# A Fourier mixing layer with one routed token, on one core: an eighth raw tile, gathered last rows, odd folds on ScalarE, one-element writes between comparisons, and a table of priorities

## The chip, the cores and the metric

The kernel runs on one core of one Trainium2 chip. The core has five engines that run their own instruction queues beside each other: TensorE (PE, matrix products; PEld is its weight load), VectorE (DVE), ScalarE (ACT), GpSimd (POOL) and SyncE (SP, which only issues transfers here). Transfers are moved by 16 DMA engines that all queues share. The metric is the device time of one launch in microseconds (us), lower is better; the figure to beat is the median of three runs.

## The reference

Everything is float32. `x` is 2048 x 576, the two sequence matrices are 2048 x 2048 (cosine and sine), the two hidden ones 576 x 576, and the three weights of the feed-forward part are 576 x 4608.

```python
def _A_ref(x, seq_re, seq_im, hid_re, hid_im):          # Fourier mixing
    a = einsum("bsd,ed->bse", x, hid_re)
    b = einsum("bsd,ed->bse", x, hid_im)
    return einsum("ts,bse->bte", seq_re, a) - einsum("ts,bse->bte", seq_im, b)

def _B_ref(x, w_r, w_gate, w_up, w_down):               # one routed token
    r = x @ w_r
    idx = argsort(-r)[:, :1]                             # the token with the highest score
    x_sel = take(x, idx)
    y = (silu(x_sel @ w_gate) * (x_sel @ w_up)) @ w_down
    y = y * sigmoid(r[idx])
    return x + scatter(zero, idx, y)

h = x + _A_ref(layernorm(x), ...)
out = h + _B_ref(layernorm(h), ...)
```

The matrices are inputs, and the kernel may not assume that they are cosines and sines. It computes the product by their symmetries (a mirrored half), and checks on the chip that the symmetries hold for the matrices it was given; if they don't, a general path at the end runs (it does not run here).

## The kernel before

**Stages.** Sixteen slots of 128 tokens lie in `X`. Stage one folds each pair of slots k and 16-k into sums and differences along the hidden axis (`fold_d`, DVE), takes the layer norm's statistics (`measure` on ACT, `ends`, `totals`, `biases` on POOL, `scales` on DVE), and brings the pair together and normalizes it by two matmuls with diagonal matrices (`diag` on DVE, `fold` on PE). `folded` writes the result from PSUM to `XF`: the even half on ACT, the odd half on DVE (L548). Stage two (`seq`, PE) multiplies `XF` by the sequence matrices, in two groups of row blocks, five products for each group; `keep` turns the sums into `Z`. Stage three (`hid`, PE) multiplies `Z` by the hidden matrices. `residual` (DVE) adds x, `spread_of` (ACT) and `dot_h` (DVE) take the second norm and the router's score, `scores` finishes a batch of blocks, `result` writes the rows that are not routed, and `store` sends them out. Then comes the token: the highest score is found over all rows (`argmax`), its row is spread to all partitions (`to_all`, `normalized`), and the weights of the feed-forward part are streamed past it. `products` on DVE, `products_on_pool` on POOL with `sums` on ACT, and `products_only` share the gate and up weights, `down` (PE) takes the down weights. The down weights of the last three blocks are the last three loads.

**The checks.** Beside this every tile of the sequence matrices is compared with its mirror image. Direct tiles come by SP (`load_c`, L357, 576 KB each), mirrored ones by an indirect DMA of POOL (L301, 448 KB). A check (`c_check`) takes up to three comparisons on DVE: `off_s` (L375, 128x896, twice) and `off_t` (L380, 128x1152); `off_h` (L387) compares halves within the resident tiles `D0`, `D1`, `D2`. Each writes differences to one of two buffers `Q`, and ACT squares and sums a buffer (L368). The hidden matrix is checked in the same way: `W` holds three tiles (rows 0 to 127, 128 to 255, and in tile C 33 last rows and 32 more), loaded by SP at L403 and L405, mirrored by POOL, compared by `off_w` (L422 to L427).

**Buffers.** Tiles that only a check needs go to `RAW`, seven buffers of 4.5 KB per partition, and to those units of `D0`, `D1`, `D2` that are free at the time. The diagonal matrices have a tile of their own, `DGT` (L196). A buffer is loaded again once DVE has compared what it holds. In the last stage the same memory makes 16 spots of 1152 KB for weights.

**What sets the order.** The program is recorded into a `Plan`: each step has an engine, a length in us, and the steps it depends on. `order` runs a list schedule over the lengths: an engine takes, of the steps that are ready, the one with the longest way to the end (`way`) plus a bonus (`push`). The instructions are then issued in that order, and each engine's queue keeps it on the chip whatever really comes first. Loads are issued in a fixed order on SP and on POOL, each behind the load before it.

Of the kernel before, what the change touches and what calls it, by code (L numbers as in the profile page):

```python
# [1 line left out]

# [53 lines left out]
N_RAW = 7  # L56
# [3 lines left out]
N_PLAN = 6  # L60

# [9 lines left out]
class Plan:  # L71
# [14 lines left out]

    def order(self):
        HOP = 0.15
        succ = [[] for _ in self.ops]
        for n in self.ops:  # L90
            for d in n["deps"]:
                succ[d["i"]].append(n)
        for n in reversed(self.ops):
            n["way"] = n["dur"] + n["tail"] + max((m["way"] for m in succ[n["i"]]), default=0.0)
        left = [len(n["deps"]) for n in self.ops]
        open_ = {}
        for n in self.ops:
            n["at"] = 0.0
            if not n["deps"]:
                open_.setdefault(n["eng"], []).append(n)  # L100
        free = {}
        done = []
        while any(open_.values()):
            best = None
            for eng, ns in open_.items():
                if not ns:
                    continue
                t = max(free.get(eng, 0.0), min(n["at"] for n in ns))
                n = min(
                    (n for n in ns if n["at"] <= t + 1e-9),  # L110
                    key=lambda n: (n["at"] if eng == "DMA" else -n["way"] - n["push"], n["i"]),
                )
                if best is None or t < best[0]:
                    best = (t, n)
            t, n = best
            open_[n["eng"]].remove(n)
            n["start"], n["end"] = t, t + n["dur"]
            free[n["eng"]] = n["end"]
            done.append(n)
            for m in succ[n["i"]]:  # L120
                hop = 0.0 if m["eng"] == n["eng"] else HOP
                m["at"] = max(m["at"], n["end"] + n["tail"] + hop)
                left[m["i"]] -= 1
                if not left[m["i"]]:
                    open_.setdefault(m["eng"], []).append(m)
        assert len(done) == len(self.ops)
        return sorted(done, key=lambda n: (n["start"], n["i"]))
# [15 lines left out]
def kernel(  # L143
# [37 lines left out]
    mp = main.enter_context(tc.tile_pool(name="main", bufs=1))  # L181


    ident = consts.tile([P, P], F32, name="ident")
    ones = consts.tile([P, P], F32, name="ones")
# [10 lines left out]
    DGT = mp.tile([P, N_DG * P], F32, name="diag")  # L196
# [6 lines left out]
    iw = consts.tile([P, 3], I32, name="iw")  # L203
# [4 lines left out]
    dve.memset(ones, 1.0)  # L208
# [5 lines left out]
    def index_tables():  # L214
        pool.iota(ji, pattern=[[1, P]], base=0, channel_multiplier=-1)
        pool.iota(ic, pattern=[[2 * P, NK], [1, 2]], base=2 * (P - 1), channel_multiplier=-2)
        pool.iota(iw, pattern=[[-P, 3]], base=D, channel_multiplier=-1)
# [11 lines left out]
    def unit_matrix():  # L229
# [67 lines left out]
    ctv = ct.rearrange("j p i k m -> (j p i) (k m)")  # L297

    def gather(tile, view, rows, at=0):

        pool.indirect_dma_start(  # L301
            tile, None, view, bass.IndirectOffsetOnAxis(ap=rows, axis=0), element_offset=at
        )
# [3 lines left out]
    bufp = main.enter_context(tc.tile_pool(name="bufs", bufs=1))  # L307

    def buf(b, shape, dtype, name):
        return bufp.tile(shape, dtype, tag=f"b{b}", name=name, bufs=1)  # L310

# [7 lines left out]
    RAW = buf("R", [P, N_RAW, 9, P], F32, "R")  # L319
# [51 lines left out]

    def off_s(j, i, u, n):

        o = Q[:, u % 2, n * 7 * P : (n + 1) * 7 * P].rearrange("p (k m) -> p k m", m=P)
        dve.tensor_tensor(o, C[j, i, True][:, 0:7, :], C[j, i, False][:, 7:0:-1, :], op=SIGN[i])  # L375

    def off_t(j, i, u):

        o = Q[:, u % 2, 14 * P : QW].rearrange("p (k m) -> p k m", m=P)
        dve.tensor_tensor(o, C[NK - j, i, False], C[j, i, False][:, :, ::-1], op=SIGN[i])  # L380

    def off_h(g, c, n, i, u):
# [3 lines left out]
        for k, op in enumerate((OP.subtract, OP.add)):  # L386
            dve.tensor_tensor(o[:, :, k::2, :], t[:, :, k::2, 0:HM], t[:, :, k::2, HM:P], op=op)  # L387

    def square(u, w, ps=P):
        add_square(Q[0:ps, u % 2, 0:w])  # L390
# [26 lines left out]
    def off_w(n, u):  # L417

        ps = W_ROWS[n]
        t, o = WM["ABC"[n]][0:ps], Q[0:ps, u % 2]  # L420
        re, im = W["ABC"[n]][0:ps, 0, :], W["ABC"[n]][0:ps, 1, :]
        dve.tensor_tensor(o[:, 0:D], t[:, 0:D], re[:, 0:D], op=OP.subtract)  # L422
        dve.tensor_tensor(o[:, D : 2 * D], t[:, D : 2 * D], im[:, 0:D], op=OP.add)
        o = o[:, 2 * D : 3 * D]
        dve.tensor_tensor(o[:, 0:287], re[:, 1:HD], re[:, D - 1 : HD : -1], op=OP.subtract)
        dve.tensor_tensor(o[:, 287:575], im[:, 1 : HD + 1], im[:, D - 1 : HD - 1 : -1], op=OP.add)
        dve.tensor_copy(o[:, 575:576], im[:, 0:1])  # L427

    W_ROWS = (P, P, 33)
# [109 lines left out]
    def folded(k, part):  # L539
# [7 lines left out]
        else:  # L547
            dve.tensor_scalar(XF[:, q, O0 + 1 : O0 + 288], o[:, :287], sc, None, op0=OP.mult)  # L548
# [955 lines left out]
```

## Time and profile before

| | before |
|---|---|
| three runs | 200.21, 201.22 and 205.07 us |
| median | 201.22 us |
| the profiled execution | 201.27 us |
| its span, first to last instruction | 199.2 us |
| bytes moved | 77.81 MB |
| granted TensorE clock, mean | 0.858 |

The profiled execution is 0.05 us above the median, and 2.07 us longer than its span. In the profile the line of an instruction names the helper that recorded it, so L301 is every gather and L368 every square. "SPq" and "POOLq" are the queues that issue transfers. The tenths of the page's second part are shares of 40 equal slices of 5 us.

### The profile page before, as it was taken

To read this page: it belongs to the slowest core of one execution; us is meant where nothing else is said; L and a number is where in the kernel's file an instruction comes from. 1 tells how busy PE (TensorE), PEld (TensorE's weight loads), DVE (VectorE), ACT (ScalarE), POOL (GpSimd) and SP (SyncE) were. 2 spreads that over 40 slices of the span, in tenths; PEclk is the share of its full clock that TensorE was granted. 3 is DMA by queue.
4 is the path that set the end of the run, shared out by engine and by line. 5 is a ranking of instruction groups with operands and counts; after the bars stand their busy time and mean duration, and the time that the engine had idled before them with its cause. 6 is when DMAs were issued, how large, how long until landed. Compare 5 with 4: busy or idle time off the path is not lost. (4 is left out here: it accounts for less than half of the span.)

```text
span 199.2 us, 2787 instructions
## 1 busy us (share of the span) xinstructions
PE 130.4 (65%) x758; PEld 89.9 (45%) x758; DVE 166.1 (83%) x419; ACT 140.5 (71%) x259; POOL 122.8 (62%) x134
## 2 busy tenths in 40 slices
PE   0007989999999989899999996600241444085840
PEld 0005667764767778677877774400121111043220
DVE  4389997989999859997999999999839997899410
ACT  2298863783987794799587599997629999786400
POOL 6578888495528878998870000006439999998500
PEclk9999999999999999999999999985555555555798
DMA  5999999999979999999999999999999999999991
GB/s 190 361 418 415 411 411 409 409 372 346 402 275 366 415 398 391 404 407 412 407 401 418 420 420 422 427 414 423 422 428 425 428 422 420 431 420 412 422 387 42
DMA packets 14491, 77.81 MB, mean 391 GB/s; under 512 B 1855, under 2 KB 1859, under 8 KB 11143
## 3 DMA queue, kind: packets, MB, share of 16 engines
q1 hardware_dynamic: 10463, 56.56, 70.8%
q0 software_dynamic: 4000, 21.03, 26.3%
q8 instruction: 7, 0.11, 0.2%
q14 instruction: 13, 0.11, 0.1%
q10 hardware_dynamic: 8, 0.00, 0.0%
HBM read 72.86 MB, written 6.49 MB: 398 GB/s over the span
## 5 line engine op out<-in xcount | busy, mean ns | idle before, releaser
L368 ACT ACTIVATE Q<-Q 128x2944 bf16<-128x2944 bf16 (+5 forms) x26 | 55.4, 2133 | 19.9 <-DVE Q L375 7.0
L610 PE MATMUL py<-W,Z 128*128 128x289 f32 x180 | 45.3, 408 | 2.3 <-DVE X L619 2.3
L565 PE MATMUL ps<-D,XF 128*128 128x320 f32 (+3 forms) x216 | 45.0, 408 | 1.2 <-DMA D<-in_ct_dram 0.8
L301 POOL DMA_INDIRECT R<-in_ct_dram,ic x21 | 34.1, 1625 | 14.5 <-DVE Q L375 10.5
L610 PEld LDWEIGHTS py<-W,Z 128*128 128x128 f32 x180 | 33.7, 189 | 13.6 <-issue 2.9
L565 PEld LDWEIGHTS ps<-D,XF 128*128 128x128 f32 (+1 forms) x216 | 32.1, 172 | 13.8 <-issue 2.5
L1201 POOL TENSOR_TENSOR D<-D,Z 128x1152 f32<-128x1152 f32 x8 | 20.8, 2618 | 1.2 <-SPq L1331 1.2
L667 POOL DMA_DIRECT2D out_dram<-X x1 | 0.6, 606 | 30.0 <-ACT X L661 30.0
L301 POOL DMA_INDIRECT D<-in_ct_dram,ic x11 | 16.1, 1468 | 3.4 <-issue 2.4
L498 ACT ACTIVATE junk<-X,XT 128x576 bf16<-128x576 f32 x16 | 12.4, 772 | 8.0 <-DVE W L459 6.5
L1206 ACT ACTIVATE junk<-D 128x576 bf16<-128x576 f32 x20 | 13.7, 683 | 4.0 <-POOLq L1331 2.3
L1228 PE MATMUL pd<-XF,H 128*1 128x144 f32 x80 | 5.3, 440 | 16.1 <-DVE H L1220 13.3
L537 PE MATMUL fo<-W,diag 128*128 128x288 f32 (+1 forms) x8 | 3.9, 665 | 16.4 <-DVE diag L528 16.4
L387 DVE TENSOR_TENSOR Q<-D 128x640 bf16<-128x640 f32 (+3 forms) x20 | 12.7, 691 | 1.4 <-DMA D<-in_ct_dram 1.4
L380 DVE TENSOR_TENSOR Q<-R,D 128x1152 bf16<-128x1152 f32 x10 | 13.4, 1349 | 0.0
L630 ACT ACTIVATE junk<-X,TD 128x576 bf16<-128x576 f32 x16 | 12.3, 768 | 1.5 <-DVE X L619 1.3
L375 DVE TENSOR_TENSOR Q<-R,D 128x896 bf16<-128x896 f32 x11 | 11.9, 1083 | 1.3 <-DMA D<-in_ct_dram 1.2
L661 ACT ACTIVATE X<-X,BB,UP 128x576 f32<-128x576 f32 x14 | 10.8, 855 | 2.4 <-DVE BB L642 2.4
L623 DVE SCALAR_TENSOR_TENSOR junk<-X,wr 128x576 bf16<-128x576 f32 x16 | 12.1, 754 | 0.3
L375 DVE TENSOR_TENSOR Q<-D 128x896 bf16<-128x896 f32 x11 | 11.8, 1081 | 0.0
L619 DVE SCALAR_TENSOR_TENSOR X<-py,X 128x576 f32<-128x576 f32 x16 | 11.5, 748 | 0.0
L375 DVE TENSOR_TENSOR Q<-R 128x896 bf16<-128x896 f32 x10 | 10.8, 1084 | 0.7 <-DMA R<-in_ct_dram,ic 0.7
(202 smaller groups left out, 262.5 us busy)
## 6 DMA issues: line engine op xcount, KB each, us to landing
D<-in_ct_dram SPq DMA_DIRECT2D x22, 576.0 KB
R<-in_ct_dram SPq DMA_DIRECT2D x10, 576.0 KB
D<-in_wu_dram SPq DMA_DIRECT2D x5, 1152.0 KB
D<-in_wd_dram SPq DMA_DIRECT2D x4, 1152.0 KB
R<-in_wg_dram SPq DMA_DIRECT2D x3, 1152.0 KB
D<-in_wg_dram SPq DMA_DIRECT2D x3, 1152.0 KB
out_dram<-X SPq DMA_DIRECT2D x2, 1440.0 KB
X<-in_x_dram SPq DMA_DIRECT2D x4, 576.0 KB
```

Source lines behind the costliest of these rows:

```text
L301: pool.indirect_dma_start(tile, None, view, bass.IndirectOffsetOnAxis(ap=rows, axis=0), element_offset=at)
L368: act.activation(t, t, AF.Square, accum_out=DS[0 : t.shape[0], n : n + 1])
L375: dve.tensor_tensor(o, C[j, i, True][:, 0:7, :], C[j, i, False][:, 7:0:-1, :], op=SIGN[i])
L380: dve.tensor_tensor(o, C[NK - j, i, False], C[j, i, False][:, :, ::-1], op=SIGN[i])
L387: dve.tensor_tensor(o[:, :, k::2, :], t[:, :, k::2, 0:HM], t[:, :, k::2, HM:P], op=op)
L498: act.activation(junk[:, 0:D], X[:, k, 0:D], AF.Square, bias=XT[:, n : n + 1], scale=-float(D), accum_out=VX[:, n : n + 1],)
L565: pe.matmul(cm(ZP[g, n][k % 2][p0 : p0 + m], w), XF[:, q, m0 : m0 + m], DT[g, i][:, :, k, 0:HM], start=k in (0, 1), stop=k in (6, 7),)
L610: pe.matmul(YP[GROUPS[g][c]][:, h, 0:w], Z[:, a, c * P : (c + 1) * P], w_block(a)[:, h * HD : h * HD + w], start=(a == 0), stop=(a == 4),)
L623: dve.scalar_tensor_tensor(junk2, X[:, k, 0:D], 1.0, wr, op0=OP.mult, op1=OP.mult, accum_out=TD[:, n, 0:1])
L630: act.activation(junk[:, 0:D], X[:, k, 0:D], AF.Square, bias=TD[:, n, 1:2], scale=-float(D), accum_out=VAR[:, n : n + 1],)
L1201: pool.tensor_tensor(t, t, xs.unsqueeze(1).to_broadcast([P, JW, D]), op=OP.mult)
L1206: act.activation(junk[:, 0:D], WB[w, j][:, r, :], AF.Copy, accum_out=acc[:, j + r : j + r + 1])
```

## The change

Seven things change.

1. `N_RAW` is 8. The eighth buffer (`SHARED`) also holds the diagonal matrices early in the program, so `DGT` needs no memory of its own; it is free for raw tiles after the last `fold`. With eight buffers there are four instead of three weight spots in `RAW`, 17 in all. The token's row (`hacc`) and a scratch of `argmax` move to `Q` and `Z`. The 128x128 tile of ones becomes one column, read with a step of 0.
2. The last rows of the hidden matrix (tile C, 66 half rows in use) come by an indirect DMA of POOL, direct and mirrored, with indices outside the bounds for the unused partitions. SP's two loads at L403 (33 rows) and L405 go. Five short iotas on POOL (`last_rows`) and seven instructions on DVE (`last_masks`) make the indices and signs. The comparison of tile C becomes two `scalar_tensor_tensor` (576 and 287 wide) and a two-element scale, and its square 865 instead of 1728 wide.
3. The odd half of `folded` is written by ACT for all nine entries, not by DVE.
4. Every comparison goes through `compare`, which writes one element of a scratch tile (`warm`) on DVE just ahead of the comparison: 74 such writes.
5. The sequence stage's last 64 rows are taken one row later (`HD + 1 - HM`), with `sgn` cut accordingly.
6. The plan's lengths are changed, transfers are planned in four parts per load and by queue, and loads carry a bonus of 15.
7. After the plan is built, a table of 338 numbers (`RANKS`) replaces the bonus of each step of DVE, ACT and POOL, so it decides the order in which the three engines' steps stand.

```diff
+RANKS = [
+    30.8, 81, -106.1, -37.5, -33.4, 124.9, 201.9, 15.1, -65.7, -70.9, -83.4, -77.9, -107.1, -18.3, 33.3, 9.5,
...
-N_RAW = 7
+N_RAW = 8
...
+    RAW = buf("R", [P, N_RAW, 9, P], F32, "R")
+    SHARED = N_RAW - 1
+    DGT = RAW[:, SHARED].rearrange("p k m -> p (k m)")
-    ones = consts.tile([P, P], F32, name="ones")
+    one = consts.tile([P, 1], F32, name="one")
+    ones = one.to_broadcast([P, P])
-    DGT = mp.tile([P, N_DG * P], F32, name="diag")
...
+    def compare(o, a, b, op):
+        dve.memset(warm[0:1, :], 0.0)
+        dve.tensor_tensor(o, a, b, op=op)
...
     def off_s(j, i, u, n):
-        dve.tensor_tensor(o, C[j, i, True][:, 0:7, :], C[j, i, False][:, 7:0:-1, :], op=SIGN[i])
+        compare(o, C[j, i, True][:, 0:7, :], C[j, i, False][:, 7:0:-1, :], SIGN[i])
...
+        if n in (2, 5):
+            t = W[name][:, 0, 0:D]
+            if n == 5:
+                t = WM[name] = raw(b, f"w{name}m").rearrange("p a e -> p (a e)")[:, 0:D]
+            gather(t, wr2, i5[:, n // 5 : n // 5 + 1], bounds_check=2 * D - 1, oob_is_err=False)
+            return
...
+        if n == 2:
+            dve.scalar_tensor_tensor(o[:, 0:D], t, m5[:, 0:1], re[:, 0:D], op0=OP.mult, op1=OP.subtract)
+            dve.scalar_tensor_tensor(
+                o[:, D : D + 287], re[:, 1:HD], m5[:, 0:1], re[:, D - 1 : HD : -1], op0=OP.mult, op1=OP.subtract
+            )
+            dve.tensor_scalar(o[:, D + 287 : D + 289], re[:, 0 : HD + 1 : HD], m5[:, 1:2], None, op0=OP.mult)
+            return
...
-            dve.tensor_scalar(XF[:, q, O0 + 1 : O0 + 288], o[:, :287], sc, None, op0=OP.mult)
+            act.activation(XF[:, q, O0 + 1 : O0 + 288], o[:, :287], AF.Copy, scale=sc)
...
-    hacc = DGT[:, 0 : D + 3]
+    hacc = QT[:, 2 * JW * D : 2 * JW * D + D + 3]
...
-    for n in range(0, N_RAW - 1, 2):
+    for n in range(0, N_RAW, 2):
         spot([n, n + 1], (RF, n), (RF, n + 1))
...
+    movable = [n for n in plan.ops if n["eng"] in ("DVE", "ACT", "POOL")]
+    assert len(movable) == len(RANKS)
+    for n, push in zip(movable, RANKS):
+        n["push"] = push
```

Three places show what this does to the order. The first is ACT at the end of the folding stage. In these rows `XF` is written by `folded` (from PSUM tiles fo and fe), `Q` by the square of a check, and `os` is the first step of `keep`, which needs a finished product of the sequence stage. Before:

```order
L546 ACTIVATE XF<-fo_315,BE 128x288
L546 ACTIVATE XF<-W,BX,RX 128x288 x2
L546 ACTIVATE XF<-fe_349,BE 128x288
L546 ACTIVATE XF<-fo_370,BE 128x288
L368 ACTIVATE Q,DS<-Q 128x2304 x2
L579 ACTIVATE os_0_422<-ps_0_1_392 128x320
L368 ACTIVATE Q,DS<-Q 128x2944
```

and now (fe_324 and fo_347 are the even halves of entries 4 and 5, the sixth and seventh of the nine that a product of the sequence stage takes in turn):

```order
L638 ACTIVATE XF<-fo_378,BE 128x288
L638 ACTIVATE XF<-fe_362,BE 128x288
L449 ACTIVATE Q,DS<-Q 128x1152
L449 ACTIVATE Q,DS<-Q 128x2944
L638 ACTIVATE XF<-fe_324,BE 128x288
L638 ACTIVATE XF<-fo_347,BE 128x288
L449 ACTIVATE Q,DS<-Q 128x2944 x2
L671 ACTIVATE os_0_478<-ps_0_1_446 128x320
```

Before, all folds stood ahead of the first square; now four squares (two of 128x2304 stand a few rows further up) stand ahead of the last two folds.

The second place is DVE in the middle of the checks, where the mirrored hidden matrix is compared. `R` and `D` are raw tiles, `Z` is the second step of `keep`. Before:

```order
L375 TENSOR_TENSOR Q<-R 128x896
L380 TENSOR_TENSOR Q<-R,D 128x1152
L583 SCALAR_TENSOR_TENSOR Z<-ps_2_0_467,os_2_501 128x5x64 x2
L583 SCALAR_TENSOR_TENSOR Z<-ps_3_0_489,os_3_521 128x5x64 x2
L375 TENSOR_TENSOR Q<-R,D 128x896
L380 TENSOR_TENSOR Q<-R,D 128x1152
```

and now:

```order
L456 TENSOR_TENSOR Q<-R 128x896
L675 SCALAR_TENSOR_TENSOR Z<-ps_1_0_467,os_1_520 128x5x64 x2
L455 MEMSET warm 1x1
L456 TENSOR_TENSOR Q<-R,D 128x1152
L455 MEMSET warm 1x1
L456 TENSOR_TENSOR Q<-R,D 128x896
```

A one-element write now stands between any two comparisons, and the steps of `keep` stand later among the checks.

The third place is SP's queue of loads from the first sequence tiles on. Before:

```order
L357 DMA D<-in_ct_dram 128x1152 x10
L357 DMA R<-in_ct_dram 128x1152 x2
L357 DMA D<-in_ct_dram 128x1152
L403 DMA W<-in_wt_dram 128x2x576 x2
L403 DMA W<-in_wt_dram 33x2x576
L405 DMA W<-in_wt_dram 32x576
L357 DMA D<-in_ct_dram 128x1152
L357 DMA R<-in_ct_dram 128x1152 x3
```

and now:

```order
L438 DMA D<-in_ct_dram 128x1152 x10
L438 DMA R<-in_ct_dram 128x1152 x3
L493 DMA W<-in_wt_dram 128x2x576 x2
L438 DMA D<-in_ct_dram 128x1152
L438 DMA R<-in_ct_dram 128x1152 x3
L438 DMA D<-in_ct_dram 128x1152 x5
```

One more raw tile is loaded ahead of the hidden matrix, and the two small loads are gone from SP.

More of the change, by code (lines that the diff above doesn't have):

```diff
@@ L99, in order @@
+        left = [len(n["deps"]) for n in ops]
+        at = [0.0] * len(ops)
+        coming = {n["eng"]: [] for n in ops}
+        ready = {e: [] for e in coming}
+        free = dict.fromkeys(coming, 0.0)
+        for n in ops:
             if not n["deps"]:
[L100 to L103, printed above, removed]
+                heappush(coming[n["eng"]], (0.0, n["i"]))
+        queue, done = None, []
+        while True:
@@ L116, in order @@
[L116 to L118 removed]
+            for eng, wait in coming.items():
+                if ready[eng]:
+                    t = free[eng]
+                elif wait:
+                    t = max(free[eng], wait[0][0])
+                else:
+                    continue
+                if best is None or t < best[0]:
+                    best = t, eng
+            if best is None:
+                break
@@ new lines, in order @@
+            t, eng = best
+            wait, now = coming[eng], ready[eng]
+            while wait and wait[0][0] <= t + 1e-9:
+                i = heappop(wait)[1]
+                heappush(now, (0.0 if eng == "DMA" else -ops[i]["way"] - ops[i]["push"], i))
+            if eng == "DMA":
+                pick = min(now, key=lambda k: (ops[k[1]]["queue"] == queue, k[1]))
+                now.remove(pick)
+                heapify(now)
+            else:
+                pick = heappop(now)
+            n = ops[pick[1]]
@@ L119, in order @@
+            end = n["end"] = t + n["dur"]
+            n["start"] = t
+            if eng == "DMA":
+                queue = n["queue"]
+            if eng != "COME":
+                free[eng] = end
             done.append(n)
             for m in succ[n["i"]]:
[L121 to L125, printed above, removed]
@@ L207 @@
     pool.memset(orow, 0.0)
-    dve.memset(ones, 1.0)
+    dve.memset(one, 1.0)
     dve.memset(eps, EPS)
@@ L751, in spread_wr @@
         for h in range(2):
-            pe.matmul(t[:, h, 0:HD], ones[0:1, :], wr[0:1, half(h)], start=True, stop=True)
+            pe.matmul(t[:, h, 0:HD], one[0:1, :].to_broadcast([1, P]), wr[0:1, half(h)], start=True, stop=True)
     def copy_wr():
@@ L781 @@
             e = last = [
-                add("ACT", 0.55, then(folded, k, 0), BIAS[k]), add("DVE", 0.3, then(folded, k, 1), MEAS[k])
+                add("ACT", 0.56, then(folded, k, 0), BIAS[k]), add("ACT", 0.56, then(folded, k, 1), MEAS[k])
             ]
@@ L820, in c_half @@
         n = [
-            add("DVE", 0.16 + 0.62 * m, then(off_h, g, c, m, i, u), [d for _, d in cus[i]], w)
+            add("DVE", 0.14 + 0.6 * m, then(off_h, g, c, m, i, u), [d for _, d in cus[i]], w)
             for i in range(2)
@@ L827, in c_half, with squares @@
         squares(u, 9 * m * P, n)
-    def squares(u, w, n, ps=P):
-        SQUARES.append(add("ACT", 0.3 + w / 1200, then(square, u, w, ps), n))
+    def squares(u, w, n):
+        SQUARES.append(add("ACT", 0.25 + w / 1220, then(square, u, w), n))
         qs.users[u].append(SQUARES[-1])
@@ L838, in c_check @@
         u1, d1 = CU[j, i, True]
-        n = [add("DVE", 1.08, then(off_s, j, i, u, 0), d0, d1, w)]
+        n = [add("DVE", 1.0, then(off_s, j, i, u, 0), d0, d1, w)]
         users[u0] += n
@@ L919, in hid_step @@
         ks = slots_of(j)
-        res = [add("DVE", 0.83, then(residual, j, k), pe_last) for k in ks]
+        res = [add("DVE", 0.68, then(residual, j, k), pe_last) for k in ks]
         ys.users[y0] += res
@@ L923, in hid_step @@
         RES[j] = [add("ACT", 0.9, then(spread_of, k), r, push=EARLY[g]) for k, r in zip(ks, res)]
-        DOT[j] = [add("DVE", 0.83, then(dot_h, k), r, ws, push=DOT_PUSH) for k, r in zip(ks, res)]
+        DOT[j] = [add("DVE", 0.68, then(dot_h, k), r, ws, push=DOT_PUSH) for k, r in zip(ks, res)]
         for js in BATCHES:
```

173 lines of the change are left out of this document (97 added, 76 removed), and 21 rows, old and new, of the table RANKS.

## Prediction, written before the changed kernel was run

> **What bounds the kernel now.** I read the page's slices first, then the table of stretches with the transfer rate, then the end in the timeline, and only then who waits for whom. The slices:
>
> ```profile
> span 199.2 us, 2787 instructions
> DMA  5999999999979999999999999999999999999991
> q1 hardware_dynamic: 10463, 56.56, 70.8%
> q0 software_dynamic: 4000, 21.03, 26.3%
> ```
>
> The 16 DMA engines are busy nearly throughout, with one hole around 55 to 60 us: the kernel is bound by its 77.81 MB, a quarter of which POOL's gathers bring (the software queue). So I ask in which stretch the rate falls. The last number of a row is GB/s, the one before it the DMA share, and the third busy column is DVE:
>
> ```profile
> 10.00:40.00 30.00, 22.66 (x82) 16.33 (x83) 27.32 (x101) 21.94 (x47) 23.33 (x61) 1.00 1.02 412
> 40.00:48.00 8.00, 8.00 (x48) 4.36 (x46) 7.48 (x13) 4.97 (x8) 5.73 (x3) 1.00 1.04 344
> 54.00:61.00 7.00, 7.00 (x27) 4.66 (x26) 7.00 (x10) 6.05 (x10) 2.44 (x3) 1.00 0.85 308
> 61.00:65.00 4.00, 4.00 (x18) 3.08 (x17) 4.00 (x4) 2.77 (x6) 3.70 (x2) 1.00 0.99 363
> 73.00:76.00 3.00, 3.00 (x15) 2.64 (x14) 1.15 (x2) 1.36 (x2) 2.11 (x3) 1.00 1.04 351
> 76.00:105.00 29.00, 28.48 (x140) 22.29 (x141) 27.81 (x45) 22.74 (x30) 24.94 (x13) 1.00 1.01 406
> 105.00:190.00 85.00, 42.11 (x326) 25.74 (x322) 74.36 (x212) 66.41 (x145) 43.79 (x31) 0.68 1.01 422
> ```
>
> Where gathers and SP's loads run together the rate is about 410 (412 and 406); four stretches lie below. Their losses against 410 are 8 x (1 - 344/410) = 1.3 us at 40 to 48, 7 x (1 - 308/410) = 1.7 at 54 to 61, 4 x (1 - 363/410) = 0.5 at 61 to 65 and 3 x (1 - 351/410) = 0.4 at 73 to 76: 3.9 us in all. At 40 to 48 and 73 to 76 the engines are busy all the same (share 1.04); only 54 to 61 has true idle time (0.85).
>
> The end shows how much of this can come out:
>
> ```profile
> 149.68 2.62 POOL L1201 TENSOR_TENSOR XF<-XF,Z 128x1152 f32<-128x1152 f32 x1 [2.90 <-ACT Z L1076]
> 184.59 2.62 POOL L1201 TENSOR_TENSOR D<-D,Z 128x1152 f32<-128x1152 f32 x1 [1.25 <-SPq L1331]
> 189.53 0.16 DVE L1220 TENSOR_TENSOR H<-hs,U 128x4 f32<-128x4 f32 x1
> 192.24 1.16 PE L1228 MATMUL pd<-W,H 128*1 128x144 f32 x32 [0.94 <-SPq L1331]
> ```
>
> The last product with down weights waits for its load until 192.24; its other input, `H`, is there at 189.69. And `H` itself comes after 14 products on POOL that start with the token's row at 149.68 and wait 1.25 us for a load at 184.59. Without that wait `H` would be there at 188.44, 3.8 us before the load. So the transfers are the end by 3.8 us; a gain beyond that needs the token earlier as well.
>
> **Why the rate falls at 54 to 65.** The gathers on POOL, the comparisons on DVE beside them, and what SP's queue waits for:
>
> ```profile
> 22.59 1.07 POOL L301 DMA_INDIRECT R<-in_ct_dram,ic  x1 [0.16 <-issue]
> 21.92 0.45 DVE L459 SCALAR_TENSOR_TENSOR D<-X 128x288 f32<-128x288 f32 x1
> 22.30 0.45 DVE L466 TENSOR_TENSOR D<-X 128x287 f32<-128x287 f32 x1
> 58.39 1.82 POOL L301 DMA_INDIRECT R<-in_ct_dram,ic  x1 [4.25 <-DVE Q L375]
> 61.75 5.58 POOL L301 DMA_INDIRECT D<-in_wt_dram,iw  x1 [0.30 <-issue]
> 61.89 1.35 DVE L380 TENSOR_TENSOR Q<-R,D 128x1152 bf16<-128x1152 f32 x1
> 65.43 1.09 DVE L375 TENSOR_TENSOR Q<-R,D 128x896 bf16<-128x896 f32 x1
> 67.20 1.09 DVE L375 TENSOR_TENSOR Q<-R 128x896 bf16<-128x896 f32 x1 [0.68 <-DMA R<-in_ct_dram,ic]
> SPq L357 <- DVE Q L375: 29.1, 9, 7.1
> ```
>
> Two things come together. POOL (4.25 us) and SP (29.1 us in nine waits) wait for `off_s` to set a buffer free: seven buffers are too few while DVE has no idle time (7.00 of 7.00). And the gather at 61.75 takes 5.58 us through five comparisons in a row, ending at 67.33, 0.8 after the last of them (66.52); at 22.59, between folds of alternating kinds, a gather takes 1.07. So comparisons back to back keep a gather from being written, and a short instruction of another kind between them seems to let it through.
>
> The Trainium skill (SBUF — State Buffer, "SBUF: two separate sides") says that VectorE and GpSimd share a port by a lock held for a whole instruction, and its next section that the loser is blocked until that instruction ends plus about 115 ns. By that a gather would lose one comparison at most, 1.35 us, and writes between comparisons would open nothing. The trace disagrees, with 5.58 us through five of them; what the rule would make of the time is the second rival.
>
> **The change part by part.** DVE, its prices first:
>
> ```profile
> L548 DVE TENSOR_SCALAR XF<-fo 128x287 f32<-128x287 f32 x7 | 3.1, 446 | 0.0
> L548 DVE TENSOR_SCALAR XF<-W,RX 128x287 f32<-128x287 f32 x2 | 0.6, 360 | 0.0
> L422 DVE TENSOR_TENSOR Q<-D,W 33x576 bf16<-33x576 f32 x1 | 0.7, 737 | 0.0
> L425 DVE TENSOR_TENSOR Q<-W 33x287 bf16<-33x287 f32 x1 | 0.4, 444 | 0.0
> L249 DVE SCALAR_TENSOR_TENSOR ux<-ux,r0x 128x4 f32<-128x4 f32 x3 | 0.5, 162 | 0.1
> L211 DVE MEMSET pm<- x1: 59/59/59, 1.2 to 1.2; 64x1 f32 x1
> ```
>
> The odd folds leave: 7 x 0.446 + 2 x 0.360 = 3.8 us. The last rows' comparison drops one 576-wide and one 287-wide pass (0.74 + 0.44 = 1.2). The masks add 7 x 0.16 = 1.1. The 74 writes have no row between comparisons; the nearest is the memset of 59 ns, the dearest small instruction the dependent one of 162, so 4.4 to 12.0 us. A write depends on nothing but the write before it, so I take 4.4 (less than nothing is excluded, what it opens is counted with the gathers). Net +0.5 us on DVE, up to +8.
>
> The place counts more than the sum. Some 25 writes (1.5 us) and the masks fall before 61 us, but so do the 3.8 us of odd folds, and two steps of `keep` stand later: DVE reaches the checks at 54 to 65 about 1 to 3 us earlier. The eighth buffer adds one tile, 0.59 MB or 1.4 us of transfers. Together 2.4 us or more against a hole of 1.7. I take it as closed, and the gather's 0.5 at 61 to 65 with it: **2.2 us**.
>
> At 40 to 48 the hidden matrix's tiles arrive in pieces of 2304 bytes, which are still loaded so; I take none of the 1.3. Of the 0.4 at 73 to 76 I take half, **0.2**. Bytes: the last rows fall from 148.5 + 72 KB direct to 148.5 KB, 0.07 MB, **0.2 us** at 410 GB/s. On POOL the added gather costs about 1.07, the row above, hidden where POOL waits for buffers (4.25); without that cover it delays the gathers behind it by that. The iotas stand where POOL waits for x rows; uncovered they cost less than a gather. SP has two loads fewer.
>
> Loads of weights start behind the checks, in buffers that come free a little earlier; the 17th spot is 1.18 MB, 2.8 us at 422. It buys nothing while the share is 1.01 there, and covers a later token.
>
> ACT and PE:
>
> ```profile
> L546 ACT ACTIVATE XF<-fo,BE 128x288 f32<-128x288 f32 x4 | 2.0, 502 | 1.9 <-PE fo L537 1.7
> 33.44 0.50 ACT L546 ACTIVATE XF<-fo,BE 128x288 f32<-128x288 f32 x1 [0.56 <-PE fo L537]
> L368 ACT ACTIVATE Q<-Q 128x2304 bf16<-128x2304 bf16 x4 | 8.5, 2124 | 2.6 <-DVE Q L387 2.6
> L368 ACT ACTIVATE Q<-Q 128x2944 bf16<-128x2944 bf16 x14 | 37.2, 2654 | 14.4 <-DVE Q L375 7.0 <-DVE Q L380 6.4 <-issue 1.0
> L368 ACT ACTIVATE Q<-Q 128x1152 bf16<-128x1152 bf16 x1 | 1.1, 1148 | 0.0
> 33.24 16.12 PE L565 MATMUL ps<-D,XF 128*128 128x320 f32 x76
> 122.60 5.11 PE L610 MATMUL py<-W,Z 128*128 128x289 f32 x20 [1.74 <-DVE X L619]
> 127.07 0.75 DVE L623 SCALAR_TENSOR_TENSOR junk<-X,wr 128x576 bf16<-128x576 f32 x1
> 138.53 0.76 DVE L623 SCALAR_TENSOR_TENSOR junk<-X,wr 128x576 bf16<-128x576 f32 x1
> 140.39 0.16 DVE L260 TENSOR_REDUCE gt<-R 128x1 f32<-128x16 f32 x1
> ```
>
> ACT gets nine odd folds, 9 x 0.50 = 4.5 us, and ahead of its last two folds the squares, 2 x 2.12 + 1.15 + 2.65 = 8.0: 12.5 us behind the old end at 33.94, less the pauses it had there (0.56 and 1.9 stand in these rows). I take 9 to 11. The first product takes its nine entries in turn, 0.42 us each (76 records in 16.12 us, two to a matmul), so the sixth, which needs entry 4, came at 33.24 + 5 x 0.42 = 35.3 and now comes at about 44. PE's chain of products ended at 122.60 + 5.11 = 127.71; it moves by some 9 us, less the few it spends waiting (1.74 in its last row): 133 to 136. Behind it stand the last residual, its square, the root and the scores; two of these are DVE passes like the 0.75 above, one an ACT pass of that size, so about 3.5 us with the small ones. The token's search then starts at 137 to 140, against 140.39 now, where it waited for 12 late `dot_h` on DVE (first and last of them quoted). So PE's late start costs nothing as long as it stays within what DVE leaves, and 3.8 us beyond that before `H` sets the end. DVE itself, 0.5 us longer and with less waiting for loads, stays near 140; with the dear writes (+8) it would come to 148 less its pauses, and decide.
>
> The sum: 2.2 + 0.2 + 0.2 = 2.6 us; 201.27 - 2.6 = **198.7 us**, 2.5 below the median of 201.22 (the profiled execution is 0.05 above that).
>
> **The rivals.** All dips close, those at 40 to 48 and 73 to 76 too, since gathers and loads then alternate: 3.9 + 0.2, 197.2 us. For it: the share there is 1.04, not short of work; against it: the 2304-byte pieces stay.
>
> The writes open nothing and only cost: gathers are let in at the end of any comparison, and the 5.58 us has another cause. DVE is then 1.5 us later at the hole, the buffer gives 1.4, the hole stays, and only the 0.2 of bytes is left: 201.1 us. For it: DVE is full from 54 to 65. Against it: the 1.07 us gather between folds. The Trainium skill's page named above has it this way.
>
> More than forecast: if gathers among comparisons are what holds the whole mixed stage back, then the 37.3 MB of 10 to 105 us (rate by length, the table's rows with 48 to 54 and 65 to 73 taken at 410) need 88.4 us at 422 instead of 95: 6.6 us, 194.5 us. Against it: 412 at 10 to 40, where hardly a comparison runs.
>
> Slower: PE's late start. The folds of entries 4 and 5 stand behind squares, and the squares behind DVE and its loads. If the sixth matmul comes at 52 or later (8 us more than I take), the scores come after 144.2 and the token, not the loads, sets the end; at 55 it is 204 us. For it: PE has only about 3.5 us of pauses to give from 35 to 128.
>
> **How the numbers follow.** Chances: the forecast 0.47, all dips 0.15, nothing opened 0.20, the raised rate 0.08, the late PE 0.10. The range takes in all but most of the raised rate and the upper half of the late PE, 196.0 to 203.0 us. Two per cent, about what a measurement of this kernel can tell from no change, is below 197.2 or above 205.2: faster is the raised rate, half of all dips and a little of the forecast, 0.20; slower is the late PE's far half, 0.05; within is 0.75. The forecast's own range is 197.6 to 199.8.
>
> **What would show it.** Right: no slice of the DMA row below 9 between 5 and 190 us, no gather over 2.5 us, the last load about 2.5 us earlier, `H` well ahead of it. Odd folds show as ACT rows of 0.5 us, the first product of the sequence stage with a pause before its sixth matmul. Wrong: writes that cost over 0.1 us each, gathers as long as before, a last product with down weights that waits for DVE's `H`, not for a load, or weights' loads that wait for the buffers of `XF` after 115 us.

## The result: slower by 1.3 per cent, and the profile after

The changed kernel takes 203.68 us (median of 6 runs, 202.23 to 204.29), the kernel before beside it 201.25 us: a ratio of 1.013, with a 95% interval of 1.009 to 1.017. The profiled execution took 203.54 us, its span is 201.9. The forecast was 198.7 us.

The page's slices after, 5.05 us each:

```profile
span 201.9 us, 2852 instructions
...
DMA  6999999999999999999967999999999999999970
...
DMA packets 14464, 77.76 MB, mean 385 GB/s; under 512 B 1889, under 2 KB 1893, under 8 KB 11114
```

The hole at 55 to 60 us is gone, and a new one stands at 101 to 111 us. To weigh them against each other, here is the table of stretches with longer stretches, the last number GB/s as before. First the kernel before, then the changed one:

```profile
10.00:76.00 66.00, 57.45 (x233) 40.37 (x234) 59.66 (x148) 48.73 (x81) 48.15 (x75) 1.00 1.00 387
76.00:99.00 23.00, 22.48 (x97) 17.96 (x97) 21.81 (x35) 17.72 (x22) 20.54 (x9) 1.00 1.02 407
99.00:114.00 15.00, 15.00 (x83) 11.07 (x82) 15.00 (x24) 10.66 (x21) 4.40 (x5) 1.00 1.01 411
114.00:190.00 76.00, 33.11 (x286) 19.00 (x284) 65.36 (x199) 60.76 (x133) 43.79 (x31) 0.64 1.01 423
```

```profile
10.00:76.00 66.00, 51.16 (x192) 34.74 (x193) 57.84 (x181) 49.94 (x84) 50.27 (x72) 0.92 1.02 409
76.00:99.00 23.00, 21.70 (x94) 17.31 (x92) 18.37 (x39) 12.90 (x17) 9.40 (x8) 1.00 1.02 409
99.00:114.00 15.00, 10.76 (x37) 8.46 (x38) 13.88 (x33) 10.33 (x18) 2.20 (x2) 0.77 0.77 275
114.00:190.00 76.00, 45.28 (x340) 30.02 (x339) 65.28 (x202) 61.31 (x132) 40.51 (x30) 0.73 1.01 420
```

Up to 76 us the change moves 66 x (409 - 387) = 1.45 MB more, which at 410 GB/s is 3.5 us won, more than the 2.4 that the forecast took there (2.2 and 0.2; its other 0.2 is for bytes). From 99 to 114 it moves 15 x (411 - 275) = 2.04 MB less, 5.0 us lost; the rest is 0.05 MB won and 0.23 lost. The sum is 0.77 MB or 1.9 us behind, against 2.27 us between the two profiled executions. So the gain came, and the transfers more than gave it back in one place. What the end itself waits for comes below, with the table.

That place in the timeline of the changed kernel, with start and length in us, and in brackets what the engine waited for ahead of the row. SP's queue, DVE, PE:

```profile
69.10 10.55 SPq L438 DMA_DIRECT2D D<-in_ct_dram  x5
79.70 6.42 SPq L438 DMA_DIRECT2D R<-in_ct_dram  x3
86.17 0.43 SPq L438 DMA_DIRECT2D D<-in_ct_dram  x1
106.62 0.33 SPq L1267 DMA_DIRECT2D R<-in_wg_dram  x1
109.58 0.33 SPq L1267 DMA_DIRECT2D R<-in_wu_dram  x1
```

```profile
90.36 0.06 DVE L455 MEMSET warm<- 1x1 f32 x1
94.78 2.37 DVE L456 TENSOR_TENSOR Q<-R,D 128x1152 bf16<-128x1152 f32 x2 [4.36 <-DMA R<-in_ct_dram]
...
100.65 0.75 DVE L711 SCALAR_TENSOR_TENSOR X<-py,X 128x576 f32<-128x576 f32 x1
```

```profile
34.33 2.85 PE L657 MATMUL ps<-D,XF 128*128 128x320 f32 x10
44.18 24.89 PE L657 MATMUL ps<-D,XF 128*128 128x320 f32 x98 [6.99 <-ACT XF L638]
...
103.24 7.36 PE L702 MATMUL py<-W,Z 128*128 128x289 f32 x20 [5.54 <-DVE X L711]
110.44 11.97 PE L657 MATMUL ps<-D,XF 128*128 128x256 f32 x72
122.34 19.77 PE L702 MATMUL py<-W,Z 128*128 128x289 f32 x80
...
194.86 2.14 PE L1322 MATMUL pd<-D,H 128*1 128x144 f32 x64 [0.73 <-DVE H L1314]
```

DVE's comparison `off_t` of slot 6 stands for 4.36 us until the direct tile of slot 10 lands at 94.78. That tile was loaded by the first of the three `R` loads at 79.70, 15.1 us earlier. On SP it stands behind four resident tiles (slots 6, 7, 0, 8 of the second matrix, into `D0`; the last four of the five `D` loads at 69.10), which PE wants only at 110. While DVE stands, its comparisons give no buffer back; the first load of weights is issued at 106.62. From 102 to 109 us the rate is 174 GB/s, and from 105 to 107 next to nothing is in transit. A residual that PE needs stands behind the waiting comparison, so PE pauses 5.54 us as well, and its chain of products ends at 122.34 + 19.77 = 142.11. At the end, the last product with down weights waits for `H`, no longer for its load.

The kernel before at the same place, on DVE. There the tile of slot 10 is wanted first by an `off_s`:

```profile
92.32 1.07 DVE L375 TENSOR_TENSOR Q<-R,D 128x896 bf16<-128x896 f32 x1
94.58 1.09 DVE L375 TENSOR_TENSOR Q<-R,D 128x896 bf16<-128x896 f32 x1 [1.19 <-DMA D<-in_ct_dram]
```

DVE comes to it at 92.32 + 1.07 = 93.39 us and waits 1.19. In the changed kernel DVE is there 3 us earlier, and the tile lands when it did (94.78 against 94.58).

And the token's search, the first step on DVE behind the last scores, which started at 140.39 before:

```profile
147.22 0.16 DVE L346 TENSOR_REDUCE gt<-R 128x1 f32<-128x16 f32 x1
```

The other rows that the prediction names. The gathers and the writes, grouped:

```profile
L388 POOL DMA_INDIRECT R<-in_ct_dram,ic x21 | 25.3, 1202 | 19.6 <-DVE warm L455 15.8 <-issue 3.4 <-DVE junk L715 0.3
...
L388 POOL DMA_INDIRECT D<-in_ct_dram,ic x11 | 14.6, 1328 | 3.5 <-issue 2.3 <-DVE Q L456 0.7 <-DMA D<-in_ct_dram,ic 0.3
...
L455 DVE MEMSET warm<- 1x1 f32 x74 | 4.4, 59 | 0.0
```

No gather takes over 2 us. A write lasts 59 ns, but lies almost wholly beside the comparison behind it: two comparisons of 896 in a row start 1.01 to 1.02 us apart, before 1.00 to 1.01.

### The profile page after: what moved, and what is told of

Its sections match the earlier page's. It is cut to its first block, busy times and chain, and to the rows that moved or that the text cites. A ratio compares the mean times of both kernels' runs of the same rounds, so it can differ in the third digit from the quotient of the medians.

```text
span 201.9 us, 2852 instructions
## 1 busy us (share of the span) xinstructions
PE 135.2 (67%) x758; PEld 93.5 (46%) x758; DVE 165.3 (82%) x489; ACT 142.8 (71%) x268; POOL 112.2 (56%) x140
## 3 DMA queue, kind: packets, MB, share of 16 engines
q0 software_dynamic: 4096, 21.18, 26.2%
## 5 line engine op out<-in xcount | busy, mean ns | idle before, releaser
L388 POOL DMA_INDIRECT R<-in_ct_dram,ic x21 | 25.3, 1202 | 19.6 <-DVE warm L455 15.8
L456 DVE TENSOR_TENSOR Q<-R,D 128x896 bf16<-128x896 f32 (+1 forms) x24 | 28.2, 1197 | 5.3 <-DMA R<-in_ct_dram 4.6
L456 DVE TENSOR_TENSOR Q<-D 128x640 bf16<-128x640 f32 (+5 forms) x32 | 26.7, 874 | 2.0 <-DMA D<-in_ct_dram 1.0
L761 POOL DMA_INDIRECT out_dram<-X,ix x3 | 3.1, 1029 | 42.6 <-ACT X L753 42.0
L1322 PE MATMUL pd<-D,H 128*1 128x144 f32 x160 | 8.4, 378 | 12.9 <-DVE H L1314 12.9
L629 PE MATMUL fo<-W,R 128*128 128x288 f32 (+1 forms) x8 | 4.2, 706 | 17.6 <-DVE R L620 17.6
L1295 POOL TENSOR_TENSOR D<-D,Z 128x1152 f32<-128x1152 f32 x6 | 15.7, 2634 | 0.0
L1322 PEld LDWEIGHTS pd<-D,H 128*1 128x1 f32 x160 | 4.5, 103 | 16.4 <-DVE H L1314 14.5
L1300 ACT ACTIVATE junk<-D 128x576 bf16<-128x576 f32 x14 | 9.6, 683 | 1.6 <-POOL D L1295 1.0
L1295 POOL TENSOR_TENSOR R<-R,Z 128x1152 f32<-128x1152 f32 x3 | 7.8, 2622 | 2.8 <-ACT Z L1170 2.8
```

Source lines behind the costliest of these rows:

```text
L388: pool.indirect_dma_start(tile, None, view, bass.IndirectOffsetOnAxis(ap=rows, axis=0), element_offset=at, **bound)
L456: dve.tensor_tensor(o, a, b, op=op)
L1295: pool.tensor_tensor(t, t, xs.unsqueeze(1).to_broadcast([P, JW, D]), op=OP.mult)
L1322: pe.matmul(T["pd"][at(h), :QD], H[:, j : j + 1], WB["d", j0][:, r, h * QD : (h + 1) * QD], start=(j == 0), stop=(j == NJ - 1),)
```

## Experiments

Most kernels here take the order that the planner made for the changed kernel and move single steps within the queue of one engine, and nothing else: `ahead(engine, steps, other)` puts the steps just ahead of the other. A load is named by its function, buffer, slot, matrix and whether it is mirrored. Ratios are to the kernel before, run on the same chip. In most of them lines beyond L840 stand five lines lower.

### The two loads on SP, swapped

```diff
+first = [("load_c", 7, 10, 0, False), ("load_c", 2, 9, 0, False)]
+ahead("SP", named("SP", *first), named("SP", ("load_c", None, 6, 1, False)))
```

> The changed kernel with two loads on SP moved: the two tiles that DVE's comparisons want at 90 to 97 us go ahead of the four resident tiles that PE wants only after 110. Theory B: DVE's wait at 90 to 95 us falls from 4.4 us to under 1, the hole at 99 to 109 us shrinks by about 4 us, and the time is 199.5 to 201. Theory A: the hole stays, since XF is freed by PE at about 122 us as before, and the time is 202.5 to 204.

Measured: 199.93 us (10 runs), 0.996 (0.992 to 1.000). And once more in more rounds:

> The changed kernel with the two loads swapped, once more, in five rounds: 199.3 to 200.5, and a ratio to the kernel before of 0.990 to 0.998.

Measured: 199.23 us (6 runs), 0.991 (0.987 to 0.994). The second run's SP queue, its PE, and its stretches:

```profile
69.74 3.09 SPq L438 DMA_DIRECT2D R<-in_ct_dram  x2
74.05 5.94 SPq L438 DMA_DIRECT2D D<-in_ct_dram  x4
...
102.22 0.33 SPq L1272 DMA_DIRECT2D R<-in_wg_dram  x1
```

```profile
98.85 5.11 PE L702 MATMUL py<-W,Z 128*128 128x289 f32 x20 [0.93 <-DVE X L711]
...
131.17 5.11 PE L702 MATMUL py<-W,Z 128*128 128x289 f32 x20 [0.57 <-DVE X L711]
```

```profile
10.00:76.00 66.00, 50.39 (x191) 34.35 (x192) 58.33 (x183) 50.70 (x86) 50.31 (x78) 0.95 1.02 410
...
99.00:114.00 15.00, 15.00 (x78) 11.98 (x80) 14.93 (x36) 10.90 (x20) 0.00 (x0) 1.00 1.00 382
114.00:190.00 76.00, 43.46 (x356) 26.85 (x356) 63.30 (x201) 60.05 (x135) 43.24 (x31) 0.69 1.01 423
```

The wanted tile is issued ten microseconds earlier, DVE does not wait for a load between 85 and 105 us, and 99 to 114 us runs at 382 GB/s in place of 275. PE's pause for the residual falls from 5.54 to 0.93 us, and its chain of products ends at 131.17 + 5.11 = 136.28 in place of 142.11. Two loads changed places, and the loss of 2.4 us became a gain, of 1.2 us in the first run (its interval reaches 1.000) and of 2.2 in the second. That the place of this load in SP's queue makes the wait and the loss, and most of the hole, is shown.

### PE's late start

The prediction's slower rival was PE's late start. Three kernels try it. First, the step that I had named: the folds of entries 4 and 5 behind ACT's squares.

```diff
+ahead("ACT", named("ACT", ("folded", 4, 0), ("folded", 5, 0)), named("ACT", ("square", 3, 2944)))
```

> The changed kernel with one move on ACT: the last two folds go ahead of the square that starts at 40.9 us, and POOL's biases stay where they are. If the squares held the folds: the folds run at 39 to 40 us and the sixth matmul comes at 40 to 41 in place of 44.2. If POOL's biases hold them: ACT stands until about 42 us, the sixth matmul comes at 42.5 to 43.5, and the squares behind it start 1 to 3 us later. The time stays within 1 us of 203.7 either way.

Measured: 205.01 us (one run). ACT and PE there:

```profile
41.74 0.50 ACT L638 ACTIVATE XF<-fe,BE 128x288 f32<-128x288 f32 x1 [1.58 <-POOL BE L613]
```

```profile
42.78 24.40 PE L657 MATMUL ps<-D,XF 128*128 128x320 f32 x98 [5.20 <-POOL XF L613]
```

The folds wait for POOL's `biases`, which the table put behind four gathers; the squares cost 1.4 us (44.18 to 42.78). So biases and folds together:

```diff
+ahead("POOL", named("POOL", ("totals", 6, 10), ("biases", 6, 10)), named("POOL", ("load_c", 5, 14, 0, True)))
+ahead("ACT", named("ACT", ("folded", 4, 0)), named("ACT", ("folded", 8, 0)))
+ahead("ACT", named("ACT", ("folded", 5, 0)), named("ACT", ("square", 0, 2304)))
```

> The changed kernel with one thing moved: on POOL the totals and biases of entries 4 and 5 go ahead of the four gathers they stood behind, and on ACT the last two folds go ahead of the squares. Everything else keeps its order. Theory A (PE's late start is what costs): the sixth matmul of the first product comes at about 37 to 38 us in place of 44.2, the stage's products follow 6 to 7 us earlier, and the time falls by 3 to 4.5 us to 199 to 200.5. Theory B (DVE's wait for a load at 90 to 95 us is what costs, and the residual behind it): PE comes early and then waits for that residual all the same, up to about 103 us, and the time stays at 203 to 204.

Measured: 206.01 us, 1.025 (1.019 to 1.031). The pause at the sixth matmul goes, but PE then waits 6.10 us for `keep` at 50.23, and its stage ends only 1.2 us earlier; DVE waits 7.6 us for its load. This says little of PE's start, so the next one also moves what held PE: five `keep` steps ahead of squares on ACT and of comparisons on DVE, and the residuals of three pairs.

```diff
 (the three lines above)
+ahead("ACT", named("ACT", ("keep", 0, 0, 0)), named("ACT", ("square", 4, 2944)))
+ahead("DVE", named("DVE", ("keep", 0, 0, 1)), named("DVE", ("off_s", 13, 0, 5, 1)))
...
+ahead("DVE", named("DVE", ("residual", 3, 13), ("residual", 3, 3)), named("DVE", ("off_t", 6, 0, 16)))
```

> The changed kernel with the biases and folds of the first run, and beside them what held PE up there: on ACT the copies out of the first stage's products go ahead of the squares, on DVE the sums that follow them go ahead of comparisons, and the residuals of the first three pairs come earlier. SP's order of loads stays. Theory C (PE's late start costs by one way: SP's queue stands at 60 to 69 us behind a load whose tile PE holds): the stage's fifth product ends at about 61 us in place of 69.0, the load that DVE misses at 90 to 95 us is issued at about 71 to 73 in place of 79.7, DVE's wait falls under 1 us, the hole at 99 to 109 us closes to under 3 us, and the time is 197.5 to 200. Theory B (only the order of the loads on SP counts): the wait stays over 3 us and the time is 202 to 204.5.

Measured: 203.92 us, 1.015 (1.011 to 1.019). PE, SP, and whom SP waited for:

```profile
46.37 13.88 PE L657 MATMUL ps<-D,XF 128*64 128x320 f32 x64 [0.48 <-DVE warm L455]
60.17 1.23 PE L850 MATMUL wrp<-wr,one 1*128 1x288 f32 x4
```

```profile
60.27 19.24 SPq L438 DMA_DIRECT2D D<-in_ct_dram  x5
79.56 5.73 SPq L438 DMA_DIRECT2D R<-in_ct_dram  x3
```

```profile
SPq L438 <- DMA D<-in_wt_dram,i: 10.2, 1, 10.2
```

PE's first stage ends 8.8 us earlier (60.2 in place of 69.0), and it buys nothing that the ratio shows: the first resident tile now waits 10.2 us for its buffer, which holds rows of the hidden matrix until they are compared, and the tile of slot 10 behind it is issued at 79.56 as before. DVE waits 5.5 us. PE gives its lead back in pauses of 4.57 and 5.18 us for DVE, and its chain ends at 140.84. Theory C falls: PE's late start was real, and taking it away won nothing here. With the swap as well:

> The kernel beside it with the two loads swapped on SP as well. If the swap and PE's early start repair the same wait: as the better of the two alone, within 1 us (198.5 to 200). If PE's early start also brings the token's chain forward, which ends last with the swap alone by 1.5 us against the transfers: 197.5 to 199.

Measured: 199.86 us, 0.992 (0.990 to 0.995), as the swap alone (0.996 and 0.991). Now the swap with the biases and folds alone:

> The first run's moves (biases on POOL ahead of four gathers, last folds on ACT ahead of the squares) together with the swapped loads. Alone those moves cost 2.3 us. If that cost came through DVE's wait for the late load: no wait over 1 us at 85 to 100, and 199.2 to 200.4. If it came from the four gathers that now stand behind the biases: 201 to 202.5.

Measured: 200.94 us, 0.997 (0.994 to 1.000). Without the swap these moves cost 2.3 us (206.01 against 203.68), with it 1.0 to 1.7 (against 199.93 and 199.23). So by the medians a part of the cost, 0.6 to 1.3 us, came by way of the wait; a wait of 2.7 us, now at 102 to 104 us and for another tile, remains.

### The residual behind the waiting comparison

```diff
+ahead("DVE", named("DVE", ("residual", 3, 13), ("residual", 3, 3)), named("DVE", ("off_t", 6, 0, 16)))
```

> The changed kernel with two residuals moved on DVE ahead of the comparison that waits for its load at 90 to 95 us. PE's pause of 5.5 us at 98 to 103 goes, and PE's last product ends about 5 us earlier, at 137. Theory A or B where the token's chain alone sets the end: 199.5 to 201. If the transfers with their hole at 99 to 109 us end nearly as late as the token's chain: no more than 1 us is won, 202.5 to 203.5.

Measured: 202.92 us, 1.009 (1.006 to 1.012). PE's pause at 98 us goes and a pause of 5.80 us for `keep` on DVE comes at 107 to 112; the chain ends 0.9 us earlier. The transfers' hole stays, and so does the time, within a microsecond. With the biases:

> Both moves of the two runs beside it. PE's last product ends at 130 to 132 us in place of 142.1. Theory A: buffer XF comes free at 109 to 112 us in place of 122, the weights' loads fill part of the hole at 99 to 109 us, and the time is 198 to 200. Theory B: DVE still waits about 4 us at 90 to 95, the hole stays at 5 us or more, and the time is 201 to 203.

Measured: 203.80 us, 1.012 (1.008 to 1.017): above Theory B's 201 to 203, and far from Theory A's 198 to 200.

Of the kernels with the table's order, ordered by the start of the token's search. All columns but the last are of the profiled execution, which can lie up to 1.8 us from the median:

| kernel | DVE's longest wait for a load, 85 to 105 us | GB/s at 99 to 114 | token's search starts | profiled us | median us |
|---|---|---|---|---|---|
| swap (second run) | none | 382 | 141.80 | 199.25 | 199.23 |
| swap and biases | 2.7 | 340 | 143.10 | 200.82 | 200.94 |
| swap and PE early | none | 327 | 144.57 | 201.61 | 199.86 |
| PE early | 5.5 | 281 | 146.06 | 202.84 | 203.92 |
| residual early | 2.6 | 271 | 146.57 | 203.91 | 202.92 |
| the change | 4.4 | 275 | 147.22 | 203.54 | 203.68 |
| biases and residual | 3.9 | 233 | 148.01 | 204.98 | 203.80 |
| folds before square (one run) | 6.7 | 237 | 148.56 | 205.01 | 205.01 |
| biases early | 7.6 | 230 | 149.28 | 205.67 | 206.01 |

The wait orders them only roughly. The start of the search does it best: the profiled time is 56.3 to 57.7 us more in all nine, and in each the last product with down weights waits for `H`. In the changed kernel POOL's 14 products with the token run without a wait for a load, `H` is there at 194.80, and the last load has landed at 193.3 (issued at 175.14, 18.2 us to landing). So the end goes by the token: DVE's wait holds up comparisons and residuals, PE waits for these, and the last scores come late. The hole in the transfers is the wait's other effect; here it ends about 1.5 us short of setting the time.

### The writes

The kernel before with the write ahead of each comparison, and the kernel with the swap without it:

```diff
+    def compare(o, a, b, op):
+        dve.memset(warm[0:1, :], 0.0)
+        dve.tensor_tensor(o, a, b, op=op)
...
-        dve.tensor_tensor(o, C[j, i, True][:, 0:7, :], C[j, i, False][:, 7:0:-1, :], op=SIGN[i])
+        compare(o, C[j, i, True][:, 0:7, :], C[j, i, False][:, 7:0:-1, :], SIGN[i])
```

> The kernel before with one thing added: the one-element write ahead of each comparison. If the writes let gathers in: the gathers of 5.6 us at 61.8 and of 4.3 to 4.4 us at 39 and at 79 to 92 us fall to under 2.1 us. The time falls by the gathers' 0.5 us at 61 to 65 and by part of the 1.3 us at 40 to 48, to 199.7 to 200.7; with the hole at 54 to 61 still there, since that waits for buffers. If they open nothing: the gathers stay long and the time is 201 to 202.

Measured: 201.46 us, 1.000 (0.997 to 1.003). Its gathers and the stretch with the hole:

```profile
L301 POOL DMA_INDIRECT R<-in_ct_dram,ic x21 | 28.7, 1365 | 20.9 <-DVE warm L374 15.4 <-issue 2.8 <-DVE Q L375 1.5
```

```profile
88.22 4.35 POOL L301 DMA_INDIRECT R<-in_ct_dram,ic  x1 [0.30 <-issue]
```

```profile
54.00:61.00 7.00, 7.00 (x27) 4.61 (x26) 7.00 (x15) 5.54 (x10) 2.59 (x2) 1.00 0.77 273
```

The gathers are shorter by 0.26 us on average (1625 ns in the same group of the kernel before, 1365 here), and the one of 5.58 us is among three of 0.94 to 1.05. One of 4.35 stays, writes or not. The hole stays too, since POOL waits for buffers there, and the time is the same: 61 to 65 us runs at 404 GB/s in place of 363, and 54 to 61 at 273 in place of 308.

> The kernel with the two loads swapped (199.9 us), without the one-element writes between comparisons. If comparisons back to back hold gathers: gathers of 4 to 6 us return, the rate at 54 to 65 us or at 76 to 90 us falls by 10 to 20 per cent, and the time rises by 1 to 3 us, 201 to 203. If the writes open nothing: gathers stay under 2.1 us, and the time is the same or up to 1 us less.

Measured: 199.84 us, 0.987 (0.983 to 0.992). Two gathers of the sequence matrices, of 32, take over 2.1 us, the longer 2.83; the rate at 65 to 73 and 73 to 76 falls to 387 and 312. Beside the kernel with writes, in more rounds:

> The same kernel without the writes, once more, beside it. If the writes are worth nothing here: the medians differ by less than 0.5 us. If they let gathers in where it counts: it is slower by 0.8 us or more. If they only cost their time on DVE (74 times about 0.015 us): it is faster by up to 1 us.

Measured: 199.23 us, 0.989 (0.985 to 0.994), the median of the kernel with the writes to the digit; its longest gather takes 2.96 us. The writes do something to single gathers and nothing to the time. Of the kernels run, the changed one with the swap is faster than before and after, with or without the writes.

### The eighth tile, the table, and the swap in the kernel before

Seven raw tiles and 16 spots, with the swap; DVE, ACT, POOL and PE keep the order of eight up to the weights.

```diff
-N_RAW = 8
+N_RAW = 7
...
-    for n in range(0, N_RAW, 2):
+    for n in range(0, N_RAW - 1, 2):
```

> The changed kernel with the two loads swapped (199.9 us), with seven raw tiles in place of eight and one weights' spot fewer; the orders of DVE, ACT, POOL and PE up to the weights are those of the kernel with eight. If the eighth tile is what closed the hole at 54 to 65 us: the rate there falls to 300 to 370, and the time rises by 1.4 to 3 us, to 201.3 to 203. If the order closed it: the rate stays over 400 and the time at 199.4 to 200.4.

Measured: 206.37 us, 1.025 (1.022 to 1.029).

```profile
48.00:54.00 6.00, 2.72 (x5) 1.85 (x6) 2.24 (x6) 3.37 (x4) 4.73 (x9) 0.50 0.48 137
54.00:61.00 7.00, 7.00 (x28) 4.57 (x28) 6.21 (x11) 4.97 (x6) 4.45 (x4) 0.94 0.88 303
```

The hole comes back and is deeper than in the kernel before. In this order, which was made for eight tiles, the eighth tile with the spot that goes with it is worth about 6.4 us (against 199.93), more than the 1.4 to 3 expected. Then the change without its table:

```diff
-    for n, push in zip(movable, RANKS):
-        n["push"] = push
```

> The changed kernel without the table: the planner's own priorities set the order, everything else of the change stays. If the table's order is what made DVE reach the late load early and PE start late: the sixth matmul of the first product comes before 38 us, DVE waits under 2 us for a load between 85 and 100 us, and the time is 199.5 to 201.5. If the wait comes from the tile and the shorter work on DVE, whatever the order: a wait of 3 us or more and a hole after 98 us remain, and the time is 202 to 205.

Measured: 205.20 us, 1.022 (1.017 to 1.027), above both ranges expected. DVE waits 1.94 us until 97.67, and the token's search starts at 141.78, as with the swap. And yet 99 to 114 us runs at 214 GB/s, and the last product waits for its load:

```profile
196.49 1.16 PE L1322 MATMUL pd<-D,H 128*1 128x144 f32 x32 [0.93 <-SPq L1429]
```

Here the hole alone sets the end. So a late token and a hole are two ways to the same loss; what makes the hole in this order was not taken apart. By the medians the table is worth some 1.5 us to the change (205.20 against 203.68, on two chips; the intervals of the two ratios touch at 1.017). Last, the swap in the kernel before:

> The kernel before with the same two loads moved on SP ahead of the four resident tiles, and nothing else. There DVE waits 1.2 us for the first of them, at 93 to 94.6 us. If the swap only repairs what the change made worse: 200.5 to 201.7, the same as before. If it is a gain in any kernel of this kind: 199.5 to 200.3, and then most of what the changed kernel with the swap wins comes from the swap.

Measured: 202.40 us, 1.004 (1.002 to 1.007), a little slower than before. PE, which is earlier there, now waits 2.83 us for a resident tile at 97.76. The swap is no gain of its own; it is right where PE comes late and DVE early.

## Why the prediction was wrong

**The step that failed** is the sentence on DVE, that "with less waiting for loads" it "stays near 140", and with it PE's chain at 133 to 136 and the token's search at 137 to 140. DVE came to the tile of slot 10 at 90.42 us, in the kernel before at 93.39, and the tile landed at 94.78, before at 94.58: DVE waited 4.36 us for it in place of 1.19. I never asked whether this load, fixed in SP's order, would come earlier too. PE then stood 5.54 us for a residual behind that comparison, its chain ended at 142.11, and the search started at 147.22. By the prediction's own slack of 3.8 us nothing is lost until 140.39 + 3.8 = 144.2; 3.0 us beyond it make 201.27 + 3.0 = 204.3 us, and the profiled execution took 203.54. The swap of two loads takes the loss back (shown): the search starts at 141.80, and the time is 199.2 to 199.9 us against the forecast's own range of 197.6 to 199.8.

**The loads of weights** failed beside it: they were to "start behind the checks, in buffers that come free a little earlier", with the stretch from 105 us on taken over at its old rate. They start at 106.62 in place of 100.91, and 99 to 114 us falls from 411 to 275 GB/s. The sooner the matrices are in, the sooner there is nothing to load but weights, and these need buffers that DVE's comparisons give back.

**The hole at 54 to 65 us**: right, and too small. All dips up to 76 us closed, 3.5 us in place of 2.4, those at 40 to 48 among them, of which I had taken none; up to there the first rival, with 3.9, was the nearer one. The eighth tile is needed for it (137 to 303 GB/s without it at 48 to 65 us), the table is not (10 to 76 us runs at 410 without it); the other parts of the change were not taken out one by one.

**The writes**: the price was wrong on the dear side. I took 59 ns each, 4.4 us; comparisons start about 0.01 us further apart, under 1 us in all. What they open was wrong too: in the kernel before they shorten gathers and close the dip at 61 to 65 us, and the time stays (1.000, 0.997 to 1.003), with the hole at 54 to 61 us deeper beside it. The Trainium skill's rule (SBUF — State Buffer, "SBUF: two separate sides" and the section behind it) is that the loser of the shared port waits for one instruction. By rows of this case that is a gather of 0.94 and a comparison of 1.35, 2.3 us. Gathers without writes in the new order, 2.96 us at most, are not far above it; the 5.58 through five comparisons before, and the 4.35 with the writes, are. Which comparisons hold a gather through several, no run here settles.

**PE's start**: the time was right by luck, 44.18 us against about 44, and the reason wrong. The folds waited for `biases` behind four gathers on POOL, a queue whose order I had not followed for this step; its last four small operations took 4.2 us there in place of 0.65. The squares cost 1.4. The rival that hung on PE's start would have cost only from 52 us on, and taking the start 8.8 us forward at the end of the stage won nothing (shown, with and without the swap).

**The end**: a sign named for being wrong came true, a last product that waits for `H`. The slack of 3.8 us was there as worked out, and used up: POOL's first product with the token stands at 156.47 in place of 149.68, 6.8 us later. Of the signs for being right, no gather over 2.5 us came true; the slices of the DMA row did not stay at 9.

**The range** ended at 203.0, and 203.68 lies above it. The slower rival, with a chance of 0.10, had the size (204) and the end (the token, not the loads), but by a sixth matmul at 52 us or later, which came at 44.18; that part is luck. A load that arrives when it used to, while its user comes earlier, was not among the rivals.

## What to carry to other kernels

When a change makes one engine earlier, look up for each thing that the engine will then want whether it becomes earlier too: a load in a fixed queue keeps its place behind loads that are wanted later. Transfers that run ahead of the work that frees their buffers give the lead back at the next stage; so a hole that closes is worth only what the following stage can take. Before a hole is called the cause of a loss, look what the last instruction waits for: here it was the token, and in the kernel without the table a load. A queue in code order should be looked at again whenever the orders of its users have been searched.

## What the runs showed of the hardware

A load of 576 KB by SP's queue lands 15.1 us after its issue in this stretch (79.70 to 94.78), behind five loads that the queue issued in the 10.6 us before it and with POOL's gathers beside it. In the kernel with early biases the same load was issued 1.2 us earlier, at 78.52, while gathers ran earlier too, and it landed at 96.86.

POOL's smallest operations stretch while DVE compares without a pause. The last four of `biases` in the changed kernel, which took 0.19 to 0.20 us each in the kernel before at 26.2 to 26.9 us:

```profile
38.67 0.91 POOL L605 TENSOR_TENSOR BX<-MX,RX 128x4 f32<-128x4 f32 x1
39.54 1.32 POOL L611 TENSOR_TENSOR V<-V,RX 128x4 f32<-128x4 f32 x1
40.82 1.05 POOL L613 TENSOR_TENSOR BE<-BX 128x2 f32<-128x2 f32 x1
41.83 1.05 POOL L613 TENSOR_TENSOR XF<-V 128x2 f32<-128x2 f32 x1
```

Four operations on two to four elements took 4.2 us from 38.67 to 42.88, about one comparison each, with the writes in place.
